# A gated linear attention with a rational MLP on one core: alpha loaded first, k turned in 112 columns, last products by token block, GpSimd made to wait for VectorE, and a new table of steps

## The chip, the cores and the metric

One core of a Trainium2 chip runs the whole program. The time is the device time of one execution in microseconds; of several runs the median is given. A difference of about 0.5% is the smallest that the measurement of this kernel can tell from none.

## The reference

```python
for t in range(S):                                   # B, H, S, D = 4, 8, 768, 48
    state = alpha[:, :, t, :, None] * state + einsum('bhd,bhe->bhde', k[:, :, t], v[:, :, t])
    y[:, :, t] = einsum('bhd,bhde->bhe', q[:, :, t], state)
x = y.transpose(0, 2, 1, 3).reshape(B * S, H * D)    # 3072 x 384
h = x @ w_in                                         # w_in 384 x 2048, float64 in memory
P = a[0] + a[1]*h + a[2]*h**2 + a[3]*h**3
Q = 1.0 + abs(b[0])*abs(h) + abs(b[1])*h**2
out = (P / (Q + 1e-6)) @ w_out                       # w_out 2048 x 384, float64 in memory
```

## The kernel before, in words

The attention runs in 24 chunks of 128 tokens (`g` 0 to 23), six to a batch. For each chunk alpha, k and q are brought head dimension first, the running products of alpha are taken by two scans on VectorE (`suffix`, `prefix`, L445 and L457), k and q are multiplied by them (`k`, `q`), and TensorE makes the scores (`s`, L489), turns k (`kt`, L507) and, after ScalarE has emptied the scores (`se`, L496) and the turned k (`ke`, L510) and GpSimd has masked the scores (`sm`, L500), makes the output and the chunk's addition to the state (`am`, L531 and L550). VectorE adds it (`kv`, L560), GpSimd or VectorE decays it (`d`, L513). ScalarE copies the output out as the MLP's input (`xh`).

The MLP runs in 96 units (`u`). Units 0 to 9 are "plain" (256 tokens by 256 hidden columns, products on whole float32 weights, L625 and L638); units 10 to 95 are "wide" (512 tokens by 128 columns, each float32 product made of three products of split operands, 18 matmuls a unit, L652, L671 and, for the last 512 tokens, L665). A unit is `in` (two halves `in.u.0`, `in.u.1`), then a chain on ScalarE, GpSimd and VectorE: `ah`, `t1`, `q1`, `qm`, `t2`, `t3`, `ars`, `sq`, `p`, `t`, `g` (L698 to L744), for wide units the split `gh` (L747) and `gl` (L751), and then `oh` and `ol` on TensorE. `in.u` has to wait for `g.(u-3)`, since the hidden values lie in three banks in turn; `oh.u` waits for `g.u` or `gh.u`.

The weights are float64 in memory and are joined to float32 on chip: per block (`i` 0 to 7 of w_in, `o` 0 to 7 of w_out, 768 KB each) a DMA `w`, on ScalarE `abs` (L252) and mostly `sign` (L264), on VectorE `low` (L260) and `join` (L280), and later `hi` (L295) and `lo` (L300). `sign` can be done on VectorE too (L266).

Every engine executes its instructions in program order. That order is not written as loops: `Plan.add` (L36) records some 2,670 steps with an engine, a cost, the steps that must come before, and for some an alternative engine; `Plan.run` (L45) issues them in the order of a packed table, `ORDER` (L62), whose top bit chooses the alternative engine. The costs are not read when the kernel is built: what the hardware sees is the order in the table and the waits that the framework derives from the tiles that each step reads and writes. Steps marked `lock=True` are operations of VectorE that use its port to SBUF which GpSimd shares.

```python
            if s["alt"]:
                s["fn"](engines[(s["alt"] if key in self.other else s)["eng"]], *s["args"])
            else:
                s["fn"](*s["args"])
```

All DMAs but two are issued by SyncE (SP). The first two segments of alpha, k and q come in whole (`nat`, L393, 384 KB each) and are turned on TensorE (`tn`, L410) ahead of which 28 turns of the identity run (`warm`, L403); later chunks come in 4 x 2 pieces of 48 KB for each of alpha, k and q (`ld`, L386), and VectorE turns them (`ta`, `tqk`, L437 and L442).

Of the kernel before, what the change touches and what calls it, by code (L numbers as in the profile page):

```python
# [24 lines left out]
class Plan:  # L25
# [19 lines left out]
    def run(self, engines):  # L45
# [4 lines left out]
        done = set()  # L50
        for n in order:
            key = keys[n & 0x7FFF]
            s = self.steps[key]
            assert all(a in done or a not in self.steps for a in s["after"])
            if s["alt"]:
                s["fn"](engines[(s["alt"] if key in self.other else s)["eng"]], *s["args"])
            else:
                s["fn"](*s["args"])
            done.add(key)
# [3 lines left out]
    'c-jTQ17KK55CG7f*}?9wZQHhO+qUg%+7wA`+qUj%+qP}Hz4s;>W1JahA{cMbOfln4U?!N9CYqUQrkluSfr(+Fn`tJBiD',  # L63
    '(v^xh9fXXkwbwCY4!XW|<{slF4ZjnoVY@S!Pz6$!3u$Y1WukW`<dA&Kodk%v!U~%ryVtX0zU;HS<htGZ=?p2(C8UO`H%',
    'm8%;*D#SFzgCYA}s6J|q5RFm1pHM7leGsk4H+srWBVX}tqH@nPmY;ONGqwuUDliOS{J3~&I5jYZ0nFHpW*=rJ;L?#Tw@',
    't~P+wwlu>j~R_gLbBO2=8(B){xi8uDbvDcx0g&(GX_hWR<@hXYg*bIq1KcM8H;W0ZnMu6G?`3y+d6a{hS;)Z0@gHbY){',
    '+HPQuHkkL_XG+sx*!8ISi(uh5Bj#dNS)OhePr4zZ!OukCF+*{9}c$YeZhI@>8&*z~hG?Nu|v9x<~pm+f!6*rE2Cscj0G',
    '0d~B7VXm8jc35aFbHh9~gKSq@$FwvPY;OC=OtiyoT{Fo}#mS-b>{Of8JTUX^NIS(AG1KfcJZ5I#J@b!kY{G0&^UO@Q6-',
    '~HpZ3f%vILgkjGx4TrV;0(n=82hUN89Hn#Iy=oU}xh?Gse!cdF)s_2i0^pvuzVo*(|YZ?JKj?j<c`LI$OznHH$(Q+bZU',
    'kd1IE@Z|1i7Vyc>cX1yJ1cG>0jt=Skl$Nn^p%nG}~el&S)Q?uKyv~z6-^Vw{&n{BB1WmegfHlOWbw%FCSr`c*x*>`4--',  # L70
    'DcmLxj4Y=3*B$On?Gi+-EI%qzh;Luu*NPzfPbx+8}^48Xb#%b_H5{Xw!fK&3-Gt;WFkN>bJHHOJMB4(aK;WYhwVcA$Fw',
    '!Q%@KRv&c{2Zk2z{D*kg7velXAN3wzt%vKMV+hy{Z~^4oj%l3juY>_~ImMga?#?R`sd#h$PXcWmE~t5%?$xn?_>0PfnC',
    '_JMtEKbcoH5<IkTZTpZ%_M7c&V!}K7#zq5$aP!zM#T6JGx|r|wx_xisnTW6qpV%Shhh2^yVnaYbZ4ww}KG+zr5~IQ&8{',
    'Z@|PwlVJk2V5zHNWj&n-o&OCtJ`ON^Ts)1)yg(86*gaNO9n^Eo75Jijd(3DIrCsDD=f9qHZDaAQFu-iOEuYh)P6E2_Pw',
    'bwb3XErH6E86{dpKn9U>_k{U8XX37B3NhvucqdbrX5`zp|gKKd_NDN9rF)1O$qIH-TVpA4ckB(AOHcD?&QBg_<#V98gw',
    'i_@dWC-z;nleKch(l>8E98cFRK&)oFq4+Do2;}A(?WI12H9yNrlYu2g7QHQ%0<Pg2IZz4A(<c#6@yJ!9MV%sN<f=2FV&',
    '*bl#lY$7A!+sF#{Dd8EHFaqEb`<YEw-rKy|1r)uYj-BGje&RMZxta#YNgr~Hu5?7$9G1ad$FDhw4U7c``jP>>qY7*m*v',
# [49 lines left out]

PACE, T0, LEAD = 5.0, 20.0, 2.0
DMA = 0.49
SV = (1.1, 2.03, 0.67, 0.46)  # L130
IN = (1.09, 1.31)
OH = (0.722, 1.3)
WIDE = 0.232
# [3 lines left out]
    (1, "a"): (0, 1), (1, "q"): (6, 7), (1, "k"): (2, 6),  # L137
}
NNAT = 2
WARM = 28  # L140
WB = 2
GB = 3
NSC = 1
# [996 lines left out]
```

## Time and profile before

| | us |
|---|---|
| runs of the kernel | 545.26, 546.98, 548.06 (median 546.98) |
| the profiled execution | 545.37 |
| its span, first to last instruction | 543.6 |
| TensorE busy | 523.7 (96%) |
| VectorE busy | 483.4 (89%) |
| ScalarE busy | 439.5 (81%) |
| GpSimd busy | 404.0 (74%) |
| mean granted TensorE clock | 0.990 |

In the profile PE is TensorE, PEld its weight load, DVE VectorE, ACT ScalarE, POOL GpSimd, SPq and ACTq the instruction queues of SyncE and ScalarE. A line of the timeline gives the start, the length, the engine and line, what is written from what, how many instructions are merged, and in brackets the idle time before it with what ended that.

### The profile page before, as it was taken

How to read it: one execution, taken by the hardware profiler on the slowest of the kernel's cores; microseconds unless marked ns; L12 is line 12 of the kernel's file. 1: busy time of each engine (PE TensorE's matmuls, PEld its weight loads, DVE VectorE, ACT ScalarE, POOL GpSimd, SP SyncE). 2: the span in 40 equal slices, each digit the busy share in tenths (PEclk: the TensorE clock that was granted, in tenths of full speed). 3: DMA queues.
4: the chain of work that ended last, by engine and by line, in shares of the span. 5: the costliest groups of instructions: out<-in, count | busy, mean ns of one | idle time of the engine just before them, and what ended most of it. 6: DMA issues, size and time to landing. Idle time of an engine off the chain costs nothing.

```text
span 543.6 us, 11871 instructions
## 1 busy us (share of the span) xinstructions
PE 523.7 (96%) x4350; PEld 433.0 (80%) x4350; DVE 483.4 (89%) x717; ACT 439.5 (81%) x737; POOL 404.0 (74%) x377
## 2 busy tenths in 40 slices
PE   8889898999999999999999999999999999999994
PEld 8778687788788777878788887888788877889994
DVE  2989989999998899999999999998899797888872
ACT  3899798999997788768787778898877778779781
POOL 2567677899997798788578667877788675786772
PEclk9998899999999999999999999999999999999998
DMA  9959966654543535643455232442553410040001
GB/s 251 307 117 279 247 170 156 143 127 117 134 126 81 129 77 116 118 118 66 102 111 108 60 74 58 94 97 69 112 114 72 93 23 20 2 78 1 1 1 61
DMA packets 146174, 57.46 MB, mean 106 GB/s; under 512 B 133056, under 2 KB 138688, under 8 KB 146112
## 3 DMA queue, kind: packets, MB, share of 16 engines
q1 hardware_dynamic: 145824, 56.27, 44.4%
q8 instruction: 35, 0.57, 0.5%
q10 hardware_dynamic: 288, 0.39, 0.2%
q14 instruction: 27, 0.22, 0.1%
HBM read 47.98 MB, written 4.72 MB: 97 GB/s over the span
## 4 chain that ended last, share of the span: by engine, by line
PE 66%; DVE 9%; DMA 9%; SPq 9%; issue 2%; ACT 2%; POOL 1%; DVEq 0%; ACTq 0%
PE ps L652 27%; PE ps L671 22%; PE ps L665 6%; SPq L386 5%; PE ps L531 4%; DMA wo_words<-in_moe_w_out_dram 4%; PE ps L489 3%; DMA wi_words<-in_moe_w_in_dram 3%; SPq L240 2%; PE ps L638 2%; DMA raw_a<-in_alpha_dram 1%; DVE t L725 1%; DVE ps L738 1%; DVE t L721 1%; DVE t L744 1%
## 5 line engine op out<-in xcount | busy, mean ns | idle before, releaser
L652 PE MATMUL ps<-x,wi 128*128 128x512 f32 x774 | 209.6, 397 | 0.2 <-DVE t L744 0.2
L671 PE MATMUL ps<-gh_gl,wo 128*128 128x512 f32 x630 | 176.0, 400 | 0.4 <-ACT gh_gl L747 0.4
L652 PEld LDWEIGHTS ps<-x,wi 128*128 128x128 f32 x774 | 143.7, 188 | 33.1 <-DVE t L744 1.7
L710 POOL TENSOR_TENSOR qm<-qm,ah 128x512 f32<-128x512 f32 x96 | 127.3, 1326 | 30.2 <-ACT qm L707 21.6
L671 PEld LDWEIGHTS ps<-gh_gl,wo 128*128 128x128 f32 x630 | 115.4, 188 | 27.9 <-ACT gh_gl L747 0.8
L751 POOL TENSOR_TENSOR gh_gl<-t,gh_gl 128x512 fp32r<-128x512 f32 x76 | 98.9, 1302 | 33.3 <-ACT gh_gl L747 11.3
L701 ACT ACTIVATE t<-ps,coef 128x512 f32<-128x512 f32 x96 | 74.3, 774 | 15.8 <-PE ps L652 9.2
L698 ACT ACTIVATE ah<-ps 128x512 f32<-128x512 f32 x96 | 57.2, 596 | 34.0 <-PE ps L652 24.5
L735 DVE SCALAR_TENSOR_TENSOR t<-t,coef,ps 128x512 f32<-128x512 f32 x96 | 70.7, 738 | 15.1 <-ACT ps L731 14.5
L721 DVE TENSOR_TENSOR t<-t,ps 128x512 f32<-128x512 f32 x96 | 64.9, 676 | 14.6 <-ACT t L701 10.7
L728 ACT ACTIVATE ps<-qm,one_eps 128x512 f32<-128x512 f32 x96 | 66.3, 691 | 11.7 <-POOL qm L710 5.9
L725 DVE SCALAR_TENSOR_TENSOR t<-t,coef,ps 128x512 f32<-128x512 f32 x96 | 70.9, 740 | 2.0 <-ACT ah L698 0.7
L705 POOL TENSOR_SCALAR qm<-ah,bab 128x512 f32<-128x512 f32 x53 | 43.0, 811 | 37.2 <-ACT ah L698 28.7
L744 DVE SCALAR_TENSOR_TENSOR t<-ps,t 128x512 f32<-128x512 f32 x96 | 65.8, 686 | 1.9
L738 DVE SCALAR_TENSOR_TENSOR ps<-qm,ps 128x512 f32<-128x512 f32 x96 | 66.0, 687 | 0.0
L747 ACT ACTIVATE gh_gl<-t 128x512 fp32r<-128x512 f32 x86 | 53.9, 627 | 7.0 <-DVE t L744 6.7
L731 ACT ACTIVATE ps<-ps 128x512 f32<-128x512 f32 x96 | 56.0, 584 | 1.8
L665 PE MATMUL ps<-wo,gh_gl 128*128 128x384 f32 x192 | 38.0, 339 | 0.0
L445 DVE TENSOR_TENSOR_SCAN tg<-ta,ps 128x528 f32<-128x528 f32 x24 | 29.9, 1244 | 8.7 <-ACT ta L429 8.7
L472 POOL TENSOR_TENSOR tqk<-tqk,tg 128x512 f32<-128x512 f32 x22 | 29.5, 1340 | 10.2 <-ACT parts L252 9.0
L665 PEld LDWEIGHTS ps<-wo,gh_gl 128*128 128x128 f32 x192 | 34.4, 188 | 2.4 <-ACT gh_gl L747 0.3
L500 POOL TENSOR_SCALAR_AFFINE_SELECT sc<-sc 128x1024 f32<-128x1024 f32 x24 | 26.9, 1120 | 12.0 <-ACT sc L496 9.7
(114 smaller groups left out, 745.3 us busy)
## 6 DMA issues: line engine op xcount, KB each, us to landing
raw_qk<-in_q_dram SPq DMA_DIRECT2D x160, 48.0 KB, 2.1
raw_a<-in_alpha_dram SPq DMA_DIRECT2D x160, 48.0 KB, 2.1
raw_qk<-in_k_dram SPq DMA_DIRECT2D x160, 48.0 KB, 2.1
wi_words<-in_moe_w_in_dram SPq DMA_DIRECT2D x8, 768.0 KB, 7.9
wo_words<-in_moe_w_out_dram SPq DMA_DIRECT2D x8, 768.0 KB, 7.0
tv<-in_v_dram SPq DMA_DIRECT2D x24, 192.0 KB, 3.2
wr<-in_alpha_dram SPq DMA_DIRECT2D x18, 256.0 KB, 3.0
out_dram<-parts SPq DMA_DIRECT2D x60, 64.0 KB, 2.1
```

What stands on the lines that cost most here:

```text
L652: nc.tensor.matmul(h_of(u), w(key)[:, kt * FU + f % FU, :], x[:, kt, xp, :], start=(n == 0), stop=(n == len(todo) - 1),)
L665: nc.tensor.matmul(bank(T_BANKS[tt], DM), g[:, tt * P : (tt + 1) * P], w(("o", f // FU))[:, f % FU, :], start=(f == 0 and first_w), stop=( ...
L671: nc.tensor.matmul(bank(O_BANKS[dt]), w(("o", f // FU))[:, f % FU, dt * P : (dt + 1) * P], g, start=(f == 0 and first_w), stop=(f == NF - ...
L701: nc.scalar.activation(buf(s, "t1", u), h_of(u), AF.Identity, bias=a2, scale=a3)
L710: nc.gpsimd.tensor_tensor(buf(s, "qm", u), buf(s, "qm", u), buf(s, "ah", u), op=ALU.mult)
L721: nc.vector.tensor_tensor(t, t, h_of(u), op=ALU.mult)
L725: nc.vector.scalar_tensor_tensor(t, t, a1, h_of(u), op0=ALU.add, op1=ALU.mult)
L728: nc.scalar.activation(h_of(u), buf(s, "qm", u), AF.Abs_reciprocal_sqrt, bias=one_eps)
L735: nc.vector.scalar_tensor_tensor(t, t, a0, h_of(u), op0=ALU.add, op1=ALU.mult)
L738: nc.vector.scalar_tensor_tensor(h_of(u), buf(s, "qm", u), 1.0 + 1e-6, h_of(u), op0=ALU.add, op1=ALU.mult)
L744: nc.vector.scalar_tensor_tensor(t, h_of(u), 2.0, t, op0=ALU.subtract, op1=ALU.mult, reverse0=True)
L751: eng.tensor_tensor(buf(s, "gl", u).rearrange("p a b -> p (a b)"), buf(s, "t1", u), gh, op=ALU.subtract)
```

## The change

Six edits. (1) `nat` loads go out as alpha, k, q, alpha, ... instead of q, alpha, k, ..., and `warm` makes 20 turns instead of 28. (2) `prime`, a ScalarE activation on a one-column tile, is put ahead of all other ScalarE work. (3) `k_turn` and `k_evac` take 112 columns of each pair of heads instead of 128. (4) The last unit's products are issued by block of 128 tokens (`og`, `ot`), each block's copy out and store behind its own products. (5) `Plan.run` remembers the last `lock` step and makes the next GpSimd step wait for it. (6) A new `ORDER`, and new costs and limits, which take effect only through `ORDER`. The chip's instructions are otherwise the same: `WARM` and the 112 columns change sizes, (4) and (6) order, (5) waits.

```diff
+    def run(self, engines, tc):
...
+            mode = s["alt"] if key in self.other else s
+            old = len(tc.nc.cur_bb.bb.instructions)
...
+            new = tc.nc.cur_bb.bb.instructions[old:]
+            if mode["lock"]:
+                held = new[-1]
+            elif mode["eng"] == "POOL" and held is not None:
+                tc.add_manual_dep(new[0], held.name, info, reason="shared port")
+                held = None
...
-WARM = 28
+WARM = 20
...
+    KW = P - GAP
+    kts = ring("kt", NSC, [P, NC4 * KW + GAP])
...
-            nc.tensor.transpose(bank(SCB)[:, a * P : (a + 1) * P], tk[g % NQ][:, a, :], ident)
+            nc.tensor.transpose(bank(SCB)[:, a * KW : (a + 1) * KW], tk[g % NQ][0:KW, a, :], ident[0:KW, 0:KW])
...
-        nc.scalar.activation(kts[g % NSC].rearrange("p a c -> p (a c)"), bank(SCB), AF.Copy)
+        nc.scalar.activation(kts[g % NSC][:, 0 : NC4 * KW], bank(SCB, NC4 * KW), AF.Copy)
...
+    def last_out(u, tt, gx):
+        f = jobs[u][2]
+        g = buf(fast_bufs, gx, u).rearrange("p a b -> p (a b)")
+        for w in (hi, lo) if gx == "gh" else (hi,):
+            nc.tensor.matmul(
+                bank(T_BANKS[tt], DM), g[:, tt * P : (tt + 1) * P], w(("o", f // FU))[:, f % FU, :],
+                start=False, stop=gx == "gl",
+            )
...
+    add("prime", "ACT", 1.5, nc.scalar.activation, (first_act, one_eps, AF.Copy), ["one_eps"])
...
-            add(("tot", g), "POOL", 0.24, totals, (g,), [("suf", g), "halves", "consts", ("d", g - NQ)], alt=("DVE", 0.15, False))
+            add(("tot", g), "POOL", 0.24, totals, (g,), [("suf", g), "halves", "consts", ("d", g - NQ)], alt=("DVE", 0.16, True))
...
+            if u == NUA - 1:
+                for tt in range(PER):
...
+                    add(("og", tt), "PE", 0.35, last_out, (u, tt, "gh"), [("gh", u), ("lo", ("o", j))] + prev, due=at)
+                    add(("ot", tt), "PE", 0.175, last_out, (u, tt, "gl"), [("og", tt), ("ot", tt - 1), ("gl", u)], lat=0.13, due=at + 2)
```

What the two tables hold for each engine, unpacked, as far as the prediction speaks of it (`i`, `o` are weight blocks, a number the chunk, segment or unit, `x2` both halves):

```
SP   before: nat.0.q nat.0.a nat.0.k w.i1 nat.1.a nat.1.k w.i0 v.0 nat.1.q w.i2 w.o0 v.1 w.i3 ld.q.4.0 coef w.o1 ld (11 of chunk 4) v.2 w.o2 w.i4
SP   after:  nat.0.a nat.0.k nat.0.q nat.1.a w.i0 nat.1.k v.0 nat.1.q coef w.i1 v.1 ld.a.4 (2) w.i2 ld.a.4 (2) w.o0 w.i4 v.2 w.i3 w.o1 ld (5) w.o2
PE   before: warm tn.0.a tn.0.k tn.0.q tn.1.a s.0 ... am.1 in.0.1 in.1.0 s.2 in.1.1 in.2.0 kt.2 in.2.1 am.2 oh.0.0 in.3.0 oh.0.1 in.3.1 s.3 in.4x2 kt.3 oh.1x2 am.3 oh.2.0
PE   after:  warm tn.0.a tn.0.k tn.0.q tn.1.a s.0 ... am.1 in.0.1 in.1x2 s.2 in.2x2 kt.2 am.2 oh.0.0 in.3x2 oh.0.1 in.4.0 s.3 in.4.1 kt.3 oh.1x2 am.3 oh.2.0
DVE  before, kv.2 to g.2: kv.2 low.o2 t2.2 suf.4 low.i4 p.1 inv.4 t.1 pre.4 g.1 join.i4 t2.3 join.o1 t3.2 t3.3 low.o4 join.o2 low.i5 p.2 p.3 t.2 ta.5 g.2
DVE  after, kv.2 to g.2:  kv.2 g.0 low.o1 join.i3 suf.4 p.1 inv.4 t.1 pre.4 t2.2 g.1 t3.2 ta.5 low.o2 join.o1 t2.3 p.2 tqk.4 t.2 t3.3 g.2
ACT  before, to ke.2: ... t1.0 ah.0 bab cp abs.o1 se.2 t1.1 ah.1 ars.0 ke.2
ACT  after, to ke.2:  ... ah.0 t1.0 q1.0 abs.o0 sign.o0 se.2 t1.1 ars.0 abs.i4 ke.2
end  before: oh.95x2 ol.95, then four copies and stores
end  after:  og.0 ot.0 og.1 ot.1 og.2 copy.1 ot.2 copy.0 og.3 copy.2 store.0 store.1 ot.3 copy.3 store.2 store.3
```

In the new table 36 GpSimd steps get the added wait, 19 of them among the work up to unit 14 (the first is `tot.1` for `q.0`; then `sm.0` for `low.i0`, `tot.2` for `sign.i0`, `d.1` for `join.i0`, `sm.1` for `low.i1`, `q.2` for `low.i2`, `qm.0` for `join.i2`, `sm.2` for `join.o0`, `q1.1` for `low.i3`, ...); 17 fall in the 80 units after that. In the MLP's chain `q1` is done by GpSimd in 62 units instead of 53, and `gl` by VectorE in 12 instead of 10.

## Rows read from the trace of the kernel before

**Rows 1.** Stretches: us, busy us (count) of PE, PEld, DVE, ACT, POOL; clock, DMA share, GB/s.
```profile
25.00:50.00 25.00, 22.46 (x306) 20.24 (x307) 22.97 (x35) 23.07 (x35) 16.31 (x14) 0.93 0.73 201
50.00:100.00 50.00, 45.23 (x387) 38.01 (x384) 47.81 (x66) 43.74 (x57) 36.08 (x30) 0.97 0.82 197
100.00:150.00 50.00, 50.00 (x471) 40.16 (x473) 49.51 (x74) 47.53 (x77) 46.42 (x35) 1.00 0.50 123
150.00:200.00 50.00, 48.99 (x445) 38.72 (x438) 46.28 (x71) 42.40 (x72) 42.59 (x35) 1.00 0.44 103
```

**Rows 2.** Timeline of the first 16 us, some lines.
```profile
0.93 0.46 SPq L393 DMA_DIRECT2D raw_qk<-in_q_dram  x1
...
1.51 6.09 PE L403 MATMUL ps<-ident 128*128 128x128 f32 x28 [1.51 <-POOL ident masks.py:199]
...
7.43 1.91 PE L410 MATMUL ps<-ident,raw_a 128*128 128x128 f32 x16
...
9.43 1.28 ACT L429 ACT_TABLE_LOAD   x1 [9.43 <-PE ps L410]
...
11.36 1.25 DVE L445 TENSOR_TENSOR_SCAN tg<-ta,ps 128x528 f32<-128x528 f32 x1 [8.65 <-ACT ta L429]
...
15.91 1.16 PE L489 MATMUL ps<-tqk 48*128 48x128 f32 x16 [0.79 <-POOL tqk L475]
```

**Rows 3.** Timeline from 39 to 91 us, some lines of PE and DVE.
```profile
39.96 0.86 PE L531 MATMUL ps<-tqk,st_d 128*32 128x128 f32 x24 [1.72 <-ACT kt L510]
...
43.16 2.39 PE L638 MATMUL ps<-t,wo_words 128*128 128x256 f32 x6
...
43.34 0.56 DVE L560 TENSOR_TENSOR st_s<-st_d,ps 128x384 f32<-128x384 f32 x1 [0.27 <-PE ps L550]
...
60.60 0.65 DVE L744 SCALAR_TENSOR_TENSOR t<-ps,t 128x512 f32<-128x512 f32 x1
...
61.30 2.35 PE L638 MATMUL ps<-t,wo_words 128*128 128x256 f32 x6 [2.48 <-DVE t L744]
...
65.68 1.46 PE L638 MATMUL ps<-t,wo_words 128*128 128x256 f32 x6
...
90.03 2.86 PE L625 MATMUL ps<-x_whole,wi_words 128*128 128x256 f32 x12 [1.66 <-DVE t L744]
```

**Rows 4.** PE alone by stretch: us, busy us (count), granted clock, DMA share, GB/s.
```profile
62.00:63.00 1.00, 1.00 (x3) 0.50 1.00 356
```

**Rows 5.** Instructions by source line, L260 and L280: count, ns min/median/max, first and last start.
```profile
L260 DVE TENSOR_SCALAR wi_words<-wi_words x8: 539/547/1272, 12.5 to 74.5; 128x768 uint32<-128x768 uint32 x8
L260 DVE TENSOR_SCALAR wo_words<-wo_words x8: 530/721/1434, 26.3 to 98.3; 128x768 uint32<-128x768 uint32 x8
...
L280 DVE SCALAR_TENSOR_TENSOR wo_words<-wr,wo_words x3: 921/1701/2020, 28.9 to 70.5; 128x768 uint32<-128x768 uint32 x3
```

**Rows 6.** DMA in the first 30 us, and one landing time.
```profile
DMA packets 11976, 7.93 MB, mean 264 GB/s; under 512 B 9926, under 2 KB 9926, under 8 KB 11974
...
raw_qk<-in_q_dram SPq DMA_DIRECT2D x1, 384.0 KB, 3.8
```

**Rows 7.** Groups of instructions by line: busy us, mean ns, idle before.
```profile
L264 ACT ACTIVATE wo_words<-wo_words 128x768 f16<-128x768 f32 x7 | 13.7, 1960 | 0.0
...
L735 DVE SCALAR_TENSOR_TENSOR t<-t,coef,ps 128x512 f32<-128x512 f32 x96 | 70.7, 738 | 15.1 <-ACT ps L731 14.5
...
L442 DVE STREAM_TRANSPOSE tqk<-raw_qk 128x1024 f32<-128x1024 f32 x20 | 24.8, 1241 | 2.4 <-DMA raw_qk<-in_q_dram 2.4
```

**Rows 8.** Timeline of PE around one turn of k.
```profile
83.17 0.60 PE L507 MATMUL ps<-ident,tqk 128*128 128x128 f32 x4
83.61 1.46 PE L625 MATMUL ps<-x_whole,wi_words 128*128 128x256 f32 x6
```

**Rows 9.** Timeline of the end.
```profile
537.26 0.49 ACT L689 ACTIVATE parts<-ps 128x384 f32<-128x384 f32 x1 [0.59 <-ACT parts L689]
537.78 0.34 ACTq L695 DMA_DIRECT2D out_dram<-parts  x1
```

More of the change, by code (lines that the diff above doesn't have):

```diff
@@ L54, in run @@
             assert all(a in done or a not in self.steps for a in s["after"])
+            mode = s["alt"] if key in self.other else s
+            old = len(tc.nc.cur_bb.bb.instructions)
             if s["alt"]:
-                s["fn"](engines[(s["alt"] if key in self.other else s)["eng"]], *s["args"])
+                s["fn"](engines[mode["eng"]], *s["args"])
             else:
                 s["fn"](*s["args"])
+            new = tc.nc.cur_bb.bb.instructions[old:]
[3 more added lines that the diff above has]
+                tc.add_manual_dep(new[0], held.name, info, reason="shared port")
+                held = None
@@ L68 @@
[L68 to L77, printed above, removed]
@@ L954, in tile_gla_then_rational_mlp @@
         for nm in "aqk":
-            add(("nat", m, nm), "SP", DMA, load_nat, (m, nm), [("set", nm, m)], kb=1.2)
+            add(("nat", m, nm), "SP", DMA, load_nat, (m, nm), (), kb=1.45)
             for par in range(2):
@@ L960, in tile_gla_then_rational_mlp @@
                 add(("tn", m, nm, par), "PE", 0.9, turn_nat, (m, nm, par),
-                    [("nat", m, nm), "ident", "warm"] + before + ([("nat", m, "k"), ("set", "k", m)] if nm == "q" else []), lat=0.13)
+                    [("nat", m, nm), ("set", nm, m), "ident", "warm"] + before + ([("nat", m, "k"), ("set", "k", m)] if nm == "q" else []), lat=0.13)
     for g in range(NGC):
@@ L976, in tile_gla_then_rational_mlp @@
                     ov = [("tn", 0, x, p) for p in range(2) for x in ("a" if nm == "a" else "kq")]
-                    add(("ld", nm, g, qd), "SP", 2 * DMA, load_akq, (nm, g, qd), [("ta" if nm == "a" else "tqk", g - 1), ("set", nm, 0)] + ov, kb=0.32)
+                    add(("ld", nm, g, qd), "SP", 2 * DMA, load_akq, (nm, g, qd), [("ta" if nm == "a" else "tqk", g - 1), ("set", nm, 0)] + ov, kb=0.23)
         if m >= NNAT:
@@ L1066, in tile_gla_then_rational_mlp @@
                 old = [("wd", m - 1, dt) for dt in range(KT)]
+            if u == NUA - 1:
+                for tt in range(PER):
+                    prev = [("ol", u - 1), ("og", tt - 1)]
+                    old = [("ws", m - 1, dt) for dt in range(KT)]
+                    add(("og", tt), "PE", 0.35, last_out, (u, tt, "gh"), [("gh", u), ("lo", ("o", j))] + prev, due=at)
+                    add(("ot", tt), "PE", 0.175, last_out, (u, tt, "gl"), [("og", tt), ("ot", tt - 1), ("gl", u)], lat=0.13, due=at + 2)
+                    add(("wd", m, tt), "ACT" if tt % 2 else "DVE", 0.5, last_done, (nc.scalar if tt % 2 else nc.vector, tt), [("ot", tt)] + old, due=at + 3)
+                    add(("ws", m, tt), "ACT" if tt % 2 else "SP", DMA, last_store, (nc.scalar if tt % 2 else nc.sync, tt), [("wd", m, tt)], kb=0.55)
+                continue
             add(("oh", u, 0), "PE", WIDE * KT, wide_out, (u, hi, "gh"), [("gh", u), ("lo", ("o", j)), ("ol", u - 1), ("oh", u - 1, 1)] + old, due=at)
@@ L1074, in tile_gla_then_rational_mlp @@
                     add(("ws", m, dt), "SP", 4 * DMA, wide_store, (m, dt), [("wd", m, dt)], kb=1.8)
-            if f == NF - 1 and m == NSUP - 1:
-                for tt in range(PER):
-                    old = [("ws", m - 1, dt) for dt in range(KT)]
-                    add(("wd", m, tt), "ACT" if tt % 2 else "DVE", 0.5, last_done, (nc.scalar if tt % 2 else nc.vector, tt), [("ol", u)] + old, due=at + 3)
-                    add(("ws", m, tt), "ACT" if tt % 2 else "SP", DMA, last_store, (nc.scalar if tt % 2 else nc.sync, tt), [("wd", m, tt)], kb=0.7)
             continue
@@ L1104, in tile_gla_then_rational_mlp @@
     ctx.enter_context(tc.manual_schedule())
-    plan.run({"DVE": nc.vector, "POOL": nc.gpsimd, "ACT": nc.scalar})
+    plan.run({"SP": nc.sync, "DVE": nc.vector, "POOL": nc.gpsimd, "ACT": nc.scalar}, tc)
     fast.close()
```

143 lines of the change are left out of this document (77 added, 66 removed).

## The prediction

> **What bounds the kernel now.** I read the busy time by stretch first. The reader is to see two regimes. From 100 us on TensorE is busy for whole stretches at full clock, with 1.01 us idle between 150 and 200 us; only fewer or cheaper matmuls can shorten that part. Before 100 us it is not: 2.54 us idle between 25 and 50 us, 4.77 between 50 and 100, mean clocks of 0.93 and 0.97, while VectorE is busy for 22.97 of 25 and 47.81 of 50 us [rows 1]. So the opening is VectorE's, the rest TensorE's, and whatever the opening saves ahead of the point where TensorE stays full goes through to the end.
>
> The timeline shows where the opening loses. TensorE turns the identity for 6.09 us, 0.217 a turn; its first real turns start at 7.43, and the first scan only at 11.36, behind 1.28 us in which ScalarE loads a table between the turns and the first copy [rows 2]. Later TensorE stands for 1.72 us until ScalarE has copied the turned k, and for 2.48 and 1.66 us until VectorE ends a unit's chain [rows 3]. After the second of these gaps the granted clock is 0.50 [rows 4]: the lower level, 1.2 instead of 2.4 GHz, met after TensorE had stood. The view by source line shows that VectorE's port operations stretch: `low` takes 0.53 us at best and 1.27 and 1.43 at worst, `join` 0.92 and 2.02 [rows 5].
>
> **The start: alpha first, 20 warm turns, table early.** Warm ends at 1.51 + 20 x 0.217 = 5.85. The load issued first at 0.93 landed 3.8 us later, at 4.7 [rows 2, 6]; with alpha in that place it is there. Its 16 turns took 1.91 us at 0.119 each; the warm turns took 0.217, the lower level by their length [rows 2]. Some alpha turns will now run at the longer value: between 1.91 and 3.5 us, taken as 2.55, so they end at 8.4 instead of 9.34. ScalarE loaded its table from 9.43 for 1.28 us with the copy behind it [rows 2]; `prime` puts that under the wait for alpha, at no cost, since ScalarE has nothing to do before 9.43; uncovered it would cost the same 1.28. The first scan then starts at 11.36 - 0.95 - 1.28 = 9.1. The first scores are due some 2.0 us before 15.91 (between 0.95, if TensorE's turns pace them, and 2.9, if all turns ran fast).
>
> The Trainium skill says in "TensorE: Matmul & The Clock Gate", Part 4, that a transpose does not count as busy for the clock in the way a matmul does. By that the eight dropped turns take nothing from the clock and the alpha turns would end at 7.8 or so. The lengths here fall from 0.217 to 0.119 between two runs of transposes with nothing else before, which speaks against it; the sum goes by the rows.
>
> **Weights behind it.** SyncE issues one queue: a `w` moved ahead of eleven `ld` steps moves 22 DMAs behind it. In the new order some 8,640 KB lie ahead of and with `o1`. At 7.93 MB in 30 us [rows 6], with the start at 2.3, that is about 33 us for `o1`, 30 for `i3`; by my chain VectorE asks for `i3` at about 39 and `o1` at 42. So DMA is no new wait; `tqk.4`, whose pieces now come later, is also asked for later, after `g.1`.
>
> **Up to `oh.0.0`.** I followed the new order with the old durations: first output `am.0` and `am.1` each end about 2.0 us earlier. Then some is given back. `ke.2` stands on ScalarE behind `sign.o0` (1.96 us, [rows 7]), `se.2`, `t1.1`, `ars.0` with the second table load, and `abs.i4`; TensorE, done with `kt.2` at about 36.5, waits for it until 38.8, where it waited until 39.96 [rows 3]. `sq.0`, `p.0`, `t.0`, `kv.2`, `g.0` follow, and `oh.0.0` starts at 42.2 instead of 43.16: **-1.0** (bounds 0 and -2.0).
>
> **VectorE from there to `g.2`.** From the end of `kv.2` (43.9) to the end of `g.2` (61.25) it takes 17.35 us [rows 3]. Stretched in it are the two `low` and the `join` at their maxima, 0.90 + 0.73 + 1.10 = 2.7 us [rows 5], which is what the wait put on GpSimd removes. The table takes out `low.i4`, `join.i4`, `low.o4`, `join.o2`, `low.i5`, `p.3` and brings in `g.0`, `join.i3`, `tqk.4`, with `low.o1` for one of the lows: three lows 1.6 + two joins 1.85 + 0.74 less `low.o1` 0.53 go, 0.65 + 0.92 + 1.24 come [rows 3, 5, 7], net -0.85. Hence about 13.8 us from 41.5, `g.2` at 55.3. TensorE, from `oh.0.0` to the end of `am.3`, had 15.6 us of work, most at full clock, so it reaches `oh.2.0` at 58.0 and no longer waits: 61.30 becomes 58.0, a further **-2.3** (bounds -1 and -3.5).
>
> **The clock.** From 61.30 to 65.68 two groups of six ran at half clock: 4.38 us, where six take about 1.3 later [rows 3, 4]. With no gap before them that is **-1.8** (bounds 0 and -1.8).
>
> **To 90 us.** TensorE's wait of 1.66 us at 90.03 [rows 3] remains in question, with a shorter one in front of it. By the same counting VectorE reaches `g.6` at about 82 if its port operations keep their minima, and TensorE reaches `in.9.0` at 82.5: level, so any hiccup shows. I take some two thirds of the long one, **-1.0** (bounds 0 and -2). From there TensorE is full.
>
> **GpSimd's waits.** 36 steps wait; queued behind each are the next `q1`, `qm`, `k`, `sm`, and behind `qm` ScalarE's `ars` and VectorE's `p`. GpSimd is busy for 36.08 of 50 us in the opening [rows 1], and the held step is mostly waiting for other input anyway, so I cost them at nothing and only count VectorE's gain. If that cover is gone they cost up to 0.9 us each. In the later part there are 17 for over 400 us. The trace has no such wait; the nearest rows are the stretches themselves.
>
> The Trainium skill, "SBUF - State Buffer", section "Who interferes with whom", says of the shared port that whoever issues first holds it for the whole instruction and the other blocks. By that the wait swaps the loser and saves nothing by itself; rows 5 agree that the loss is up to a GpSimd instruction's length.
>
> **k in 112 columns.** Four turns take 83.61 - 83.17 = 0.44 us [rows 8], 0.11 each. If the columns set it, 14 ns go per turn, 0.055 per step, and 16 to 20 steps lie where TensorE is full: **-1.0** (bounds 0, if the weight load sets it, and -1.1). ScalarE's copy shrinks too, beside other work.
>
> **The end.** The last ScalarE copy starts at 537.26, after the other copy (0.49) and its DMA issue (0.59 idle) [rows 9]. By block, the other block's copy and issue lie under TensorE's last products: **-1.0** (bounds -1.1 and 0, if the verdict's branch and not the last store sets the end).
>
> Costs, `load_w`'s argument and the dropped waits of `nat` change no instruction: 0. The idle 1.01 us after 150 us depends on the new table; I leave it, between -1.8 and +2.
>
> **Sum.** -1.0 - 2.3 - 1.8 - 1.0 - 1.0 - 1.0 = -8.1 against the profiled execution's 545.37: 537.3. That execution lies 1.6 under the median of 546.98, so in terms of the median I say **539**.
>
> **Rivals.** *The port only swaps sides.* Now GpSimd is late: `qm`, then `ars`, `sq`, `p`. For: opening DVE and POOL are tied through that chain, and the port rule above. Against: POOL has idle time there. Then the 2.7 us to `g.2` are lost to TensorE only in part, since 58.0 is TensorE's own time, but the clock drop and the waits before 90 stay: -1.0 - 2.3 - 0.5 for the rest = -3.8 or so, 543.2. *More.* The gaps before `oh.0.0` vanish as well, and with them the half clock at 43.16 (2.39 us for six): -8.1 - 3.5, 535.4. *Slower.* In the full part the mask `sm` is queued on GpSimd behind `q1` and `qm`, now more of them (62 `q1` against 53) and partly held for VectorE; when it comes late, `am` leaves TensorE idle. It decides from 0.7 us at each of the 16 later attention steps: 11 us eat the 8.1 and 2.7 more, 549.7. For: counted in the new table with the old durations, TensorE's work between scores and output goes down to 3.3 us in places. Against: it does in the old table too, where the full part loses 1.01 us in one stretch and nothing in another [rows 1]. The change doing nothing: the openings would have to end at the same time; that is the lower edge of the first rival.
>
> **Numbers.** Forecast 0.58, swap 0.22, more 0.11, slower 0.09. What a measurement here can tell is 0.5%, 2.7 us. The forecast is faster but for a tail; half of the swap's spread reaches into 544.3 and above: faster 0.77, same 0.15, slower 0.08. The range from 533 (the bounds of the forecast and part of "more") to 546 (the swap's upper edge) leaves about 2 in 10.
>
> **What would show it.** First scan near 9.1 and first scores near 14; `low` and `join` all near their minima and no VectorE operation over 1.3; `oh.2.0` near 58 with no wait on L744 and no half clock after it; TensorE full from about 83 us; the turn of k at 0.39 for four; the last ACT copy directly behind the last product. It is wrong if GpSimd's waits for VectorE appear ahead of TensorE's gaps, if a `low` waits for its weights, or if TensorE stands for 0.7 us in each attention step after 100 us.

## The result, and the profile after

The changed kernel takes 537.86 us (median of 4 runs, from 536.46), the kernel before 547.52 beside it on the same chip (4 runs, 545.26 to 548.64). The ratio is 0.983, 95% interval 0.980 to 0.987: some 9 us, 1.7%, faster. One of the four runs took 576.92 us at a granted clock of 0.85 and is left out of the comparison; the median of the other three is 536.71. The profiled executions took 536.71 and 545.37, 8.66 us apart. Of TensorE's span of 534.9 us 520.3 are busy (97%), of VectorE 481.5, of ScalarE 430.9, of GpSimd 392.7.

The same stretches as in [rows 1]:

```profile
25.00:50.00 25.00, 20.88 (x297) 19.37 (x296) 22.15 (x33) 23.33 (x33) 9.83 (x11) 0.93 0.82 241
...
50.00:100.00 50.00, 49.34 (x466) 41.59 (x465) 49.65 (x74) 48.05 (x66) 34.45 (x33) 1.00 0.67 182
...
100.00:150.00 50.00, 50.00 (x471) 40.49 (x470) 48.61 (x74) 46.66 (x76) 46.25 (x38) 1.00 0.51 119
```

From 50 to 100 us TensorE now stands for 0.66 us instead of 4.77, at full clock, and VectorE is busy for 49.65 of 50: both are full. But 25 to 50 us has become worse, with 4.12 us idle for 2.54.

The start, which answers to [rows 2]:

```profile
1.51 4.53 PE L416 MATMUL ps<-ident 128*128 128x128 f32 x20 [1.51 <-POOL ident masks.py:199]
...
5.83 2.38 PE L423 MATMUL ps<-ident,raw_a 128*128 128x128 f32 x16
...
8.30 1.28 ACT L442 ACT_TABLE_LOAD   x1 [8.30 <-PE ps L423]
...
10.28 2.40 DVE L458 TENSOR_TENSOR_SCAN tg<-ta,ps 128x528 f32<-128x528 f32 x2 [7.65 <-ACT ta L442]
...
14.98 1.16 PE L502 MATMUL ps<-tqk 48*128 48x128 f32 x16 [1.53 <-DVE tqk L488]
```

Alpha's turns end 1.1 us earlier, at about 8.2. The table load is still where it was, between them and the first copy. A little later TensorE runs at half clock, which it did not at this place in the kernel before: behind stands of 1.53 us at 14.98 and 1.11 at 17.26 (the second fence is a window by itself: busy PE, clock, DMA share, GB/s).

```profile
17.26 1.01 PE L520 MATMUL ps<-ident,tqk 112*128 112x112 f32 x4 [1.11 <-ACT sc L509]
```

```profile
18.00:19.00 1.00, 1.00 (x7) 0.50 1.24 316
```

From the first scores to the second it takes 8.41 us (14.98 to 23.39), where it took 6.93 (15.91 to 22.84): 1.5 us are lost here.

Around the first output products, for [rows 3] (ScalarE, TensorE and VectorE in order of time):

```profile
37.55 1.28 ACT L750 ACT_TABLE_LOAD   x1
...
40.25 0.53 ACT L523 ACTIVATE kt<-ps 128x448 f32<-128x448 f32 x1
...
40.83 1.48 PE L544 MATMUL ps<-tqk,st_d 128*32 128x128 f32 x24 [2.56 <-ACT kt L523]
...
45.10 0.68 DVE L766 SCALAR_TENSOR_TENSOR t<-ps,t 128x512 f32<-128x512 f32 x1
...
45.84 1.56 PE L651 MATMUL ps<-t,wo_words 128*128 128x256 f32 x6 [1.27 <-DVE t L766]
...
58.07 0.69 DVE L766 SCALAR_TENSOR_TENSOR t<-ps,t 128x512 f32<-128x512 f32 x1
...
61.06 1.56 PE L651 MATMUL ps<-t,wo_words 128*128 128x256 f32 x6
...
85.89 1.46 PE L638 MATMUL ps<-x_whole,wi_words 128*128 128x256 f32 x6
```

TensorE stands for 2.56 us until ScalarE has copied the turned k of chunk 2; ScalarE came to it late, through its second table load and `abs.i4`. Then `am.2` runs at half clock, as the window by itself shows. The kernel before had such stretches at 41.5 to 44.9 us and at 61.9 to 65.3 [rows 4], the changed kernel has them at 17.0 to 20.4 and at 40.9 to 44.3:

```profile
41.00:42.00 1.00, 1.00 (x24) 0.50 0.62 112
```

So `oh.0.0` starts at 45.84, 2.7 us later than before. `oh.2.0` has caught up (61.06 for 61.30) and, without its gap of 2.48 us, runs at full clock: 1.56 for 2.35. From there TensorE doesn't stand, and `in.9.0` starts at 85.89 instead of 90.03, with the same products behind it.

VectorE's port operations by shape (min, median, max in ns, first and last start), for [rows 5]:

```profile
L271 DVE TENSOR_SCALAR wi_words<-wi_words x8: 518/548/916, 15.9 to 79.9; 128x768 uint32<-128x768 uint32 x8
...
L271 DVE TENSOR_SCALAR wo_words<-wo_words x8: 521/550/575, 32.5 to 95.5; 128x768 uint32<-128x768 uint32 x8
...
L291 DVE SCALAR_TENSOR_TENSOR wo_words<-wr,wo_words x3: 955/961/985, 36.9 to 67.8; 128x768 uint32<-128x768 uint32 x3
```

But for one `low` of 0.92 no `low` and no `join` is stretched. Another operation on VectorE, `sign`, took 1.35 us once, at 17.92 (1.03 to 1.19 in the kernel before):

```profile
17.92 1.35 DVE L277 TENSOR_SCALAR wi_words<-wi_words 128x768 uint16<-128x768 uint16 x1
```

The turn of k, for [rows 8]: 0.38 us from its start to the next product, where it was 0.44.

```profile
72.93 0.55 PE L520 MATMUL ps<-ident,tqk 112*128 112x112 f32 x4
...
73.31 1.47 PE L651 MATMUL ps<-t,wo_words 128*128 128x256 f32 x6
```

The end, for [rows 9] (TensorE's last products, ScalarE's last copy, its last store, and from the page's DMA issues over the last 20 us the KB and the time to landing):

```profile
528.17 2.46 PE L693 MATMUL ps<-wo,gh_gl 128*128 128x384 f32 x12
...
530.67 0.49 ACT L711 ACTIVATE parts<-ps 128x384 f32<-128x384 f32 x1 [0.55 <-PE ps L693]
...
531.19 0.34 ACTq L717 DMA_DIRECT2D out_dram<-parts  x1
...
out_dram<-parts ACTq DMA_DIRECT2D x2, 192.0 KB, 2.0
```

From the end of the last product to the end of the span it takes 534.9 - 530.63 = 4.27 us; before, 543.6 - 536.15 = 7.45.

Put together: of the 8.7 us of span between these two executions the opening up to `in.9.0` gives 4.1, the stretch from there to the last product 1.4 (the turns of k, 0.06 a chunk, and 1.49 us idle from 100 to 500 us where 1.80 were), the end 3.2. How far the opening's 4.1 is this one execution's, e3 shows below.

### The profile page after: what moved, and what is told of

It is laid out like the page before. It is cut to its first block, busy times and chain, and to the rows that moved or that the text cites. A ratio compares the mean times of both kernels' runs of the same rounds, so it can differ in the third digit from the quotient of the medians.

```text
span 534.9 us, 11861 instructions
## 1 busy us (share of the span) xinstructions
PE 520.3 (97%) x4342; PEld 430.2 (80%) x4342; DVE 481.5 (90%) x716; ACT 430.9 (81%) x730; POOL 392.7 (73%) x387
## 4 chain that ended last, share of the span: by engine, by line
PE 77%; DVE 6%; POOL 4%; ACT 4%; SPq 4%; DMA 4%; issue 1%; POOLq 0%; ACTq 0%
PE ps L665 29%; PE ps L684 23%; PE ps L678 6%; PE ps L544 6%; PE ps L651 4%; PE ps L502 4%; PE ps L638 3%; SPq L399 1%; DMA wi_words<-in_moe_w_in_dram 1%; SPq L406 1%; POOL gh_gl L773 1%; DMA tv<-in_v_dram 1%; PE ps L520 1%; PE ps L563 1%; DVE t L743 1%
## 5 line engine op out<-in xcount | busy, mean ns | idle before, releaser
L732 POOL TENSOR_TENSOR qm<-qm,ah 128x512 f32<-128x512 f32 x96 | 124.4, 1297 | 24.9 <-ACT qm L729 14.9
L773 POOL TENSOR_TENSOR gh_gl<-t,gh_gl 128x512 fp32r<-128x512 f32 x74 | 95.8, 1297 | 16.6 <-PE ps L684 5.3
L727 POOL TENSOR_SCALAR qm<-ah,bab 128x512 f32<-128x512 f32 x62 | 48.1, 776 | 48.0 <-ACT ah L720 20.6
L485 POOL TENSOR_TENSOR tqk<-tqk,tg 128x512 f32<-128x512 f32 x21 | 27.1, 1292 | 14.7 <-DVE tg L458 8.8
L678 PE MATMUL ps<-wo,gh_gl 128*128 128x384 f32 x180 | 35.1, 336 | 0.0
L678 PEld LDWEIGHTS ps<-wo,gh_gl 128*128 128x128 f32 x180 | 31.9, 188 | 2.1
```

What stands on the lines that cost most here:

```text
L678: nc.tensor.matmul(bank(T_BANKS[tt], DM), g[:, tt * P : (tt + 1) * P], w(("o", f // FU))[:, f % FU, :], start=(f == 0 and first_w), stop=( ...
L732: nc.gpsimd.tensor_tensor(buf(s, "qm", u), buf(s, "qm", u), buf(s, "ah", u), op=ALU.mult)
L773: eng.tensor_tensor(buf(s, "gl", u).rearrange("p a b -> p (a b)"), buf(s, "t1", u), gh, op=ALU.subtract)
```

## The experiments

Each kernel was run beside the kernel before on the same chip; the chips differ from group to group, so the ratios compare and the medians less so. Spans are those of single profiled executions.

| kernel | median us (runs) | ratio to before, 95% interval | span |
|---|---|---|---|
| the changed kernel | 537.86 (4) | 0.9834 (0.9801 to 0.9867) | 534.9 |
| e1 after without the waits | 547.58 (12) | 1.0016 (0.9999 to 1.0032) | 546.9 |
| e2 before with the waits | 542.77 (6) | 0.9935 (0.9915 to 0.9956) | 540.8 |
| e3 after with the old end | 541.60 (7) | 0.9924 (0.9896 to 0.9952) | 537.2 |
| e4 before with the new end | 543.73 (6) | 0.9960 (0.9944 to 0.9976) | 541.8 |
| e5 after, `prime` first | 538.21 (6) | 0.9838 (0.9812 to 0.9865) | 537.9 |
| e6 e5 with one table | 539.00 (4) | 0.9859 (0.9845 to 0.9874) | 537.3 |
| e7 after, `ars.0` behind `ke.2` | 536.32 (5) | 0.9813 (0.9793 to 0.9833) | 534.5 |
| e8 e6 and e7 | 537.45 (5) | 0.9831 (0.9817 to 0.9845) | 536.7 |
| e9 e5, four loads earlier | 536.85 (5) | 0.9828 (0.9802 to 0.9855) | 536.5 |
| e10 e5, `g.7` ahead of `ta.7` | 536.20 (5) | 0.9817 (0.9795 to 0.9839) | 534.1 |
| e11 e5, e7, e9, e10 together | 535.75 (6) | 0.9825 (0.9794 to 0.9855) | 533.8 |
| e12 e11 without e5 | 536.62 (5) | 0.9815 (0.9795 to 0.9836) | 536.3 |

**What the waits on GpSimd are worth.** e1 takes them out of the changed kernel, e2 puts them into the kernel before.

```diff
 e1, in the changed kernel (e2: the same lines, and tot on VectorE marked lock, added to the kernel before)
-            new = tc.nc.cur_bb.bb.instructions[old:]
-            if mode["lock"]:
-                held = new[-1]
-            elif mode["eng"] == "POOL" and held is not None:
-                tc.add_manual_dep(new[0], held.name, info, reason="shared port")
-                held = None
```

> The changed kernel with the same table, without the added waits of GpSimd. Theory (VectorE's stretched port operations cost the opening): some `low` and `join` stretch again to over 1.2 us, TensorE stands 2 to 5 us more before 100 us, and the time is 2 to 5 us above the changed kernel's. Rival (the wait only swaps who loses): GpSimd's gaps for VectorE vanish, VectorE stretches, and the time stays within 1 us of the changed kernel's.

Without the waits the changed kernel is no faster than the kernel before: all 9 to 10 us are gone, twice the most that the theory gave. Of e1, the stretch from 50 to 100 us, two groups by shape, and one of TensorE's waits (us, times, longest):

```profile
50.00:100.00 50.00, 45.99 (x396) 37.78 (x396) 50.00 (x69) 43.77 (x56) 34.88 (x28) 1.00 0.68 188
...
L265 DVE TENSOR_SCALAR wo_words<-wo_words x8: 515/1448/1641, 34.3 to 103.6; 128x768 uint32<-128x768 uint32 x8
...
L285 DVE SCALAR_TENSOR_TENSOR wo_words<-wr,wo_words x3: 954/1961/2045, 38.8 to 71.8; 128x768 uint32<-128x768 uint32 x3
...
PE ps L632 <- DVE wi_words L285: 1.9, 1, 1.9
```

VectorE has not one idle moment in those 50 us; a median `low` of w_out takes 1.45 us where it took 0.72 in the kernel before and takes 0.55 with the waits. In the view by line all `low` together take 14.1 us against 9.1, all `join` 21.1 against 15.2: 10.9 us more, about what the kernel loses. The granted clock does not explain the loss: the one run of e1 at a clock of 1.0 took 544.72 us, while the three compared runs of the changed kernel took 539.01 at most, at clocks of 0.993 and 0.994. The loser changes with the waits, and it matters which: GpSimd's lateness reaches TensorE directly nowhere in the changed kernel (its list of waits names GpSimd once, at the first identity), and up to 100 us the chain of work that ended last has no piece on GpSimd; VectorE's reaches it at once.

> The kernel before with its old table, with the added waits alone. Theory: `low` and `join` at their minima of 0.53 and 0.92 us, so `g.2` ends 2 to 3 us earlier than 61.25 and the time falls by 2 to 5 us. Rival (swap): the time stays within 1 us of the kernel before. A second rival (the old table was laid out without such waits, so a held step stands in the way): slower by up to 3 us.

e2 gains 3.6 us. The gap at `oh.2.0` goes, as forecast, though not every `low` and `join` is at its minimum (up to 0.89 and 1.34 us), but here GpSimd is late somewhere else, in the mask of the scores:

```profile
58.94 1.56 PE L648 MATMUL ps<-t,wo_words 128*128 128x256 f32 x6 [0.16 <-DVE t L754]
...
85.42 1.08 PE L541 MATMUL ps<-sc,tv 128*32 128x128 f32 x32 [2.44 <-POOL sc L510]
```

So the parts don't add: the waits alone bring 0.65%, all the rest with no waits nothing, both 1.7%. As e1 keeps the new end, which e3 and e4 below put at some 2 us, its opening without the waits is even slower than the old one. By the lengths above, the new table without the waits has more `low` running against a GpSimd instruction than the old one. That its order leaves GpSimd room for being held is read from where TensorE waits for GpSimd, in e2 and not in the changed kernel; no run shows it by itself.

**The end.** e3 puts the old order of the last products, copies and stores into the changed kernel, e4 the new one into the kernel before.

```diff
 e3, appended to the table in this order
+    og.0 to og.3, ot.0 to ot.3, copies 0 and 2, copy 3, store 3, copy 1, store 2, store 1, store 0
 e4, last unit
-    oh and ol over all four blocks, then four copies and stores
+    per block: its three products; copies 1, 0, 2, stores 0, 1, copy 3, store 2, store 3
```

> The changed kernel with the last unit's products part by part instead of block by block, and its copies and stores in the old order; nothing else. Theory (the end gave about 3 us, from the last product to the end of the span 4.3 us now against 7.4 before): the distance goes back to 6.5 to 7.5 us and the time up by 2 to 3 us. Rival (only the one copy and its store issue lie differently, as predicted): up by 1.0. Rival (the verdict's branch sets the end): no change.

> The kernel before with its old table, but the last unit's products by block and each block's copy and store behind them. Theory: from the last product to the end of the span 4.3 to 5 us instead of 7.4, the time 2 to 3 us down. Rival: 1.0 down. Rival (the verdict's branch): no change.

Of e3 TensorE's last products, ScalarE's last store, and time to landing; then of e4 the last products and store:

```profile
527.40 2.25 PE L709 MATMUL ps<-wo,gh_gl 128*128 128x384 f32 x12
...
531.39 0.34 ACTq L733 DMA_DIRECT2D out_dram<-parts  x1
...
out_dram<-parts ACTq DMA_DIRECT2D x2, 192.0 KB, 3.3
```

```profile
535.48 2.02 PE L682 MATMUL ps<-wo,gh_gl 128*128 128x384 f32 x10 [0.65 <-POOL gh_gl L775]
...
538.10 0.34 ACTq L719 DMA_DIRECT2D out_dram<-parts  x1
```

The distance from last product to end follows the order, not the rest of the kernel: 7.55 us in e3 (529.65 to 537.2), 4.3 in e4 (537.50 to 541.8), although e4's products wait 0.65 us for a split that GpSimd makes. It has two halves. The last store is issued 0.56 us after the last product instead of 1.63 [rows 9]: that is the 1.0 us of the forecast. And behind that issue it takes 3.7 us in the changed kernel and e4, 5.8 in the kernel before and e3. The four stores of 192 KB move at 307 to 389 GB/s for some 2.1 us in either order. Behind that a thin tail of transfers follows, until 3.7 us after the last issue in the kernel before and e3, until 2.2 after it in the changed kernel and e4. These are two slices, the first of the kernel before, 2.7 us after its last issue, the second of the changed kernel, 2.3 after its own (at the end DMA share and GB/s):

```profile
540.50:541.00 0.50, 0.00 (x0) 0.00 (x0) 0.00 (x0) 0.00 (x0) 0.00 (x0) 0.50 0.16 25
```

```profile
533.50:534.00 0.50, 0.00 (x0) 0.00 (x0) 0.00 (x0) 0.00 (x0) 0.00 (x0) 1.00 0.00 0
```

So the tail is 1.5 of the 2.1 us. Why the old order has it, and where the other 0.6 between the last transfer and the end of the span come from, no run separates. By the medians e3 loses more than the forecast 2 to 3 us, some 5; its runs spread from 538.89 to 545.57, and the profiled spans differ by 2.3.

**The start and the gap ahead of `am.2`.** `prime` did not do what I had read into it: in the new table it stands behind 376 of ScalarE's 694 steps and runs at 287.04 us for 0.19, when the table has long been loaded. e5 puts it first; e6 does so with the function of `ars`, whose table also serves the first copies, so that one load is left; e7 moves `ars.0`, which brings the second load, behind `ke.2`; e8 is both.

```diff
 e5, in ORDER
+    prime ahead of every other ScalarE step
 e6, besides
-    add("prime", "ACT", 1.5, nc.scalar.activation, (first_act, one_eps, AF.Copy), ["one_eps"])
+    add("prime", "ACT", 1.5, nc.scalar.activation, (first_act, one_eps, AF.Abs_reciprocal_sqrt), ["one_eps"])
 e7, in ORDER
-    ars.0 abs.i4 ke.2 sq.0
+    abs.i4 ke.2 ars.0 sq.0
```

> The changed kernel with `prime` moved from its place in the table (behind 376 other ScalarE steps, at 287 us) to the head of ScalarE's queue, as I had taken it to be. Theory: the table load of 1.28 us leaves 8.30, the first scan starts at 9.0 instead of 10.28, the first scores some 1.2 us before 14.98; what is left of it at 100 us is 0 to 1.3 us, since a gap of 2.56 us before `am.2` hangs on ScalarE and not on the start. Rival: the load still comes with the first copy, no change.

> The same, but the first activation is the reciprocal square root of the MLP's chain, so that the one load might bring a table that serves all later functions. Theory: only one table load in the profile; the one at 37.55 goes as well, `ke.2` ends 1.3 us earlier, TensorE's gap before `am.2` falls from 2.56 to about 1.3, half clock after it goes or stays, and the time falls by 1.3 to 3 us against the changed kernel. Rival: the copies load their own table again, two loads, as in the run above or worse by up to 1.3.

> The changed kernel with ScalarE's `ars.0`, and its table load, moved behind `ke.2` (order `abs.i4`, `ke.2`, `ars.0`, `sq.0`), nothing else. Theory (the 2.56 us gap before `am.2` and the half clock behind it are what the opening still loses, because `ke.2` is queued behind the load): the gap falls to about 0.7 us, the clock stays at its upper level, `oh.0.0` starts near 43.8 instead of 45.84, and the time falls by 1.5 to 2.5 us. Rival (VectorE sets `g.0` anyway, through `sq.0`): `oh.0.0` moves by less than 0.7 and the time by less than 0.7.

> Both edits together: one early table and `ke.2` ahead of `ars.0`. Theory: no gap over 1 us before 100 us but the first, `oh.0.0` near 42 to 43, and 2.5 to 4 us less than the changed kernel. Rival: the two remove the same gap, no better than the better one of them alone.

None of the four is clearly faster than the changed kernel. Yet the edits do what they should. In e7 the gap ahead of `am.2` is 0.63 us; but the wait for `g.0` behind it has grown from 1.27 to 2.99, and `oh.0.0` starts at 44.40, forecast 43.8. In e6 one table load is left; then TensorE stands 3.57 us at 58.03 for a `join`. e8, forecast without a gap over 1 us, has three of 2.03 to 2.46. In e5 the load runs at 0.89 us, the first scan at 8.83 (forecast of this edit in the prediction: 9.1), and `oh.0.0` starts at 41.27, 4.57 us ahead of the changed kernel. Only 1.44 of these are there at the first scores (13.54 for 14.98). Another 1.48 come from there to the second scores and 1.65 from `am.2` to `oh.0.0`: in both places e5 runs at full clock and the changed kernel at half.

By `in.9.0` 3.0 us of the lead are left (82.88 for 85.89), and the first wide product gives the rest back (92.56 for 92.18; e5, three lines of TensorE; what VectorE waited for there; what SyncE waited for between 30 and 60 us, and the same of the changed kernel in the fence after it):

```profile
37.91 0.86 PE L559 MATMUL ps<-tqk,st_d 128*32 128x128 f32 x24 [2.57 <-ACT kt L538]
...
41.27 1.56 PE L666 MATMUL ps<-t,wo_words 128*128 128x256 f32 x6 [1.28 <-DVE t L781]
...
92.56 2.47 PE L680 MATMUL ps<-x,wi 128*128 128x512 f32 x5 [2.94 <-DVE t L781]
...
DVE ta L465 <- DMA raw_a<-in_alpha_dram: 2.9, 1, 2.9
...
SPq L414 <- DMA wi_words<-in_moe_w_in_dram: 5.4, 3, 2.5
...
SPq L414 <- DMA wo_words<-in_moe_w_out_dram: 5.3, 3, 3.5
```

```profile
SPq L399 <- DVE ta L450: 8.0, 2, 5.3
```

In the changed kernel SyncE waits for VectorE to free a buffer; in e5 VectorE is ahead, and SyncE's loads wait for the weights' transfers before them. VectorE then stands 2.9 us for pieces of alpha, and TensorE for `g.7` behind that turn, and on its return it runs at half clock (2.47 us for five products that take 1.52).

How much of such a lead belongs to the edit? e3 has the very opening of the changed kernel, since only its last unit differs, and so is a second execution of it. It reached the first scores at 13.95 and the second at 20.89, without the half clock there, stood the same 2.56 us ahead of `am.2`, ran at half clock from 39 to 42 us, and started `oh.0.0` 2.8 us earlier than the changed kernel did. `in.9.0` followed at 83.08, 2.8 us earlier too. Then it stood at the first wide product as e5 did:

```profile
43.03 1.56 PE L667 MATMUL ps<-t,wo_words 128*128 128x256 f32 x6 [1.26 <-DVE t L782]
...
91.55 1.40 PE L681 MATMUL ps<-x,wi 128*128 128x512 f32 x5 [1.83 <-DVE t L782]
```

From 30 to 95 us its SyncE waited 14.0 us for the weights' transfers and 3.4 for VectorE, the changed kernel's 1.8 and 15.1. So two executions of one opening lie 2.8 us apart at `oh.0.0`, and a lead of that size in a single profile says little about an edit. The cleanest reading of `prime` is at the first scan, between executions with nearly the same warm turns: 7.93 in e6 (warm turns 3.89 us), 9.25 in e3 (3.93). Its place is worth 1.3 us there, the length of the load.

**Are the loads the floor?** The last four kernels ask whether that is one load in a bad place or the transfers as a whole.

```diff
 e9, in ORDER, besides e5
+    ld.a.7 (four steps) ahead of ld.k.6.1, where they stood 2 to 8 places of SyncE's queue behind it
 e10, besides e5
-    ta.7 g.7 t3.8
+    g.7 t3.8 ta.7
 e11: e5, e7, e9 and e10; e12: e7, e9 and e10
```

> The real first place for prime (e5) made TensorE reach the first output product 4.6 us earlier than the changed kernel (41.27 against 45.84) and oh.5.1 2.9 us earlier (88.06 against 90.96), and then it stood 2.94 us for g.7 and ran 15 products at half clock. Theory 'queue': VectorE's turn ta.7, which stands ahead of g.7, waited 2.91 us for four loads of alpha that SyncE issued last of its block (87.29 us). This kernel is e5 with those four loads (eight transfers) put ahead of the loads of k and q of step 6. Then the gap of 2.94 is below 1, the half clock behind it (2.47 + 2.76 + 2.01 us where 1.5 + 1.46 + 1.28 are usual, 3.0 us) is gone, the span is 532 to 533.5 and the ratio to before about 0.975. Rival 'transfers': the 16 DMA engines as a whole have no room up to 95 us, so another load becomes late in its place: TensorE stands as long elsewhere, span 536.5 to 538.

> e5 with the turn ta.7 put behind g.7 and t3.8 on VectorE, loads untouched. Theory 'queue': the load is as late as in e5 and VectorE still stands for it, but g.7 is done at about 88.2 instead of 92.4, so TensorE has no gap at the first wide product and no half clock: span 532 to 533.5, ratio about 0.975, unless ta.7's lateness reaches the scan of step 7 and the scores behind it (then 1 to 2 us come back later). Rival 'transfers': the gap moves to the next product that VectorE feeds, span 536.5 to 538.

> e5 with the four loads early, ta.7 behind g.7, and ars.0 behind ke.2 (e7's edit). If the queue theory holds this is the fastest of all: the gap of 2.57 us before am.2 falls to about 0.6 (as in e7), of which the wait for g.0 takes most back; span 531 to 533, ratio 0.970 to 0.976. If the opening as a whole is bound by transfers: 535 to 537, no better than e7 (534.5).

> e7 (prime left where the changed kernel has it, ars.0 behind ke.2) with the four loads early and ta.7 behind g.7. In e7 TensorE stood only 0.67 us at the first wide product, because it came there no earlier than VectorE. Both theories give little: 0.5 to 0.8 us less than e7, span 533.7 to 534.2, ratio about 0.980. Beside e11 it says what prime's place is worth once the loads are not in the way: 1 to 2.5 us by the queue theory, nothing by the rival.

In e9 the gap at the first wide product closes and opens 9 us later, where VectorE now stands for the pieces of k and q that were moved back (the bracket and the view name what came last in the queue):

```profile
98.49 1.94 PE L670 MATMUL ps<-t,wo_words 128*128 128x256 f32 x6 [2.02 <-DVE t L785]
...
DVE tqk L474 <- DMA tv<-in_v_dram: 2.5, 1, 2.5
```

`oh.0.0` starts at 43.23 in e9 and 43.24 in e10, no earlier than in e3. In e10 the first wide product starts at 89.58, 2.6 us ahead of the changed kernel; a wait of 0.76 and others follow, and by the last product 0.8 us are left of it (529.86 for 530.63). e3, whose opening is the changed kernel's own, ends that product at 529.65, so no gain can be told here.

```profile
89.58 1.51 PE L681 MATMUL ps<-x,wi 128*128 128x512 f32 x5
...
97.24 1.56 PE L667 MATMUL ps<-t,wo_words 128*128 128x256 f32 x6 [0.76 <-DVE t L782]
```

e11 has the shortest span, 533.8, above the 531 to 533 of the queue theory, and its interval takes in the changed kernel's 0.983. Beside it e12, without `prime` first, has 0.9815 for 0.9825: its place is worth nothing in the time, as the rival has it. e12's own span, forecast 533.7 to 534.2, is 536.3. In it TensorE stood 2.56 us at yet another place, 80.37, where VectorE had waited 4.0 for pieces of k. So the rival holds by and large: `oh.0.0` starts 2.6 to 6.7 us earlier than in the changed kernel in e5, e6 and e9 to e12, and 2.8 in e3 with no edit there; waits for loads, or for VectorE behind them, take most of that back before 100 us, and about 1 us at most comes out at the end. That the transfers are the cause is read from these waits; a kernel that moves fewer bytes was not tried. No version beats the changed kernel by more than the measurement tells.

## Why the prediction was right, and where it was wrong

The time, the direction and the range held: 539 forecast, 537.86 measured; 537.3 for the profiled execution, which took 536.71. Two sizes were off, and it is luck that they cancel: the opening was priced at -6.1 and gave -4.1 in this execution (in e3 -7.0 at `in.9.0`, of which it then lost 1.8 at the first wide product), the end at -1.0 and gave -3.2.

**The start and "up to `oh.0.0`" (-1.0) failed.** I took `prime` to stand first on ScalarE from its place in the code and did not look it up in the table; the account of the change above makes the same mistake. The load stayed, the first scan came at 10.28 instead of 9.1 and the first scores at 14.98 instead of 14. e3 came to 9.25 and 13.95 with the load in the same place, because its turns were shorter: the two agree with the forecast by luck. Alpha's turns, taken as 2.55 us, took 2.38 here and 1.91 to 2.67 in the other runs with 20 warm turns. Then came 1.5 us of half clock between the first and the second scores, which the sum does not have. TensorE was done with `kt.2` at 38.3 instead of 36.5 and waited 2.56 us for `ke.2` where I had 2.3. The half clock behind it, which I had only in the rival "more", cost 1.65 us up to `oh.0.0` by e5's lengths, and the wait for `g.0` 1.27. Together +2.7 instead of -1.0, and -0.1 in e3: the step fails in either.

**VectorE from there to `g.2` was right, and the clock at its place.** From the end of `kv.2`, where `g.0` starts (45.10), to the end of `g.2` (58.07 + 0.69) it took 13.7 us, forecast 13.8; from `oh.0.0` to `oh.2.0` 15.2, forecast 15.8 (0.8 less for the six products at `oh.0.0`, now at full clock); the gap and the half clock at `oh.2.0` are gone, and so is the term of 1.8 us. `in.9.0` follows 24.8 us later, forecast 24.5. In this execution all that was late is the point from which it was counted; but the clock took 1.5 us back at 17 to 20 us, where the kernel before has full clock, and e3 has full clock there with the same opening.

**The waits at nothing.** That held, and e1 shows how much hung on it. The Trainium skill says in "SBUF - State Buffer", "Who interferes with whom", that the first issuer holds the shared port for the whole instruction and the other blocks, from which I made the rival "swap". The runs agree with the rule (a blocked `low` takes up to 1.1 us longer, somewhat under a GpSimd instruction) and not with the rival: a wait that only chooses the loser is worth 10 us here. In the kernel before, e2, the rival was partly true: 3.3 us of TensorE's time go to the mask there.

**k in 112 columns (-1.0)** came as forecast in its length, 0.38 for four. Over 19 chunks 0.06 each make 1.1 us, which fits the 1.4 between `in.9.0` and the last product; no run has this edit alone. **The clock and transposes.** I had set the rows against the Trainium skill ("TensorE: Matmul & The Clock Gate", Part 4). After 20 warm turns instead of 28 the sixteen turns of alpha took 2.38 us instead of 1.91, some of them at the longer 0.217, and ended at 8.2: forecast 8.4 by the rows, 7.8 by that page. One execution can't tell the two apart: with the same 20 turns ahead of them alpha's took 1.91 us in e3, e7 and e12 and 2.67 in e9 and e10, and the 28 turns took 6.09 us in the kernel before, 5.16 in e2 and 4.69 in e4. What stands is that transposes alone bring the shorter length in every run (e12: 20 warm turns in 3.91 us, then alpha's 16 in 1.91), which does not agree with that page of the Trainium skill.

**The end (-1.0) was undersized.** The copy and issue under the products gave 1.07; that the span ends sooner behind the last issue I left out, although [rows 9] and the span show 5.8 us there. e3 and e4 show it as a term of its own, 2.1 us, 1.5 of them in the tail of the stores.

## What to carry to other kernels

Where an engine that is full shares a port with one that is not, an ordering wait on the second can be worth more than any single move in the order, but only with an order that leaves it the slack: try both, since neither alone told what the two do together. A time saved at the very start is worth what the loads behind it can follow; see whether the load queue waits for the engines or for transfers before you price it. One profile of an opening is one draw: two executions of the same one lay 2.8 us apart here, so compare several before you price an edit of the start. And a step's place is what the table says, not where the code adds it.

## What was not expected of the hardware

The same gap was not always followed by the lower clock. In e7 TensorE stood 2.99 us ahead of `oh.0.0` and went on at full clock; in e11 it stood 2.99 at the same product and went on at half (2.93 us for the same six products):

```profile
44.40 1.56 PE L667 MATMUL ps<-t,wo_words 128*128 128x256 f32 x6 [2.99 <-DVE t L782]
```

```profile
41.48 2.93 PE L673 MATMUL ps<-t,wo_words 128*128 128x256 f32 x6 [2.99 <-DVE t L788]
```

Likewise a gap of 2.56 to 2.58 ahead of `am.2` was followed by half clock in the changed kernel, in e3, e9 and e10, and by full clock in e5 (0.86 us for the 24 products, 1.48 in the changed kernel). Nor is the first rise fixed: the same 28 turns from the same start took 6.09, 5.16 and 4.69 us. So the granted clock behind one gap can't be read off its length, and a term for it, such as my -1.8, has both ends.
